# Attention and two MoE layers on one core: the second batch's x and the weight sums in finer pieces, DVE and ACT of M2(0,1) ordered by the scheduler

## The chip, the core and the metric

The kernel runs on one core of a Trainium2 chip. The core has TensorE (PE, the matrix engine), VectorE (DVE), ScalarE (ACT), GpSimd (POOL) and SyncE (SP), which here only issues DMA transfers. Each engine runs its own instructions in order and waits for the others by semaphores. The time is that of one execution on the device, in microseconds (us). The time before is 1480.57 us, the median of 3 runs (1477.91 to 1485.29).

## What is computed

The reference, cut to what matters. There are 8 batches of 576 tokens, 8 heads of 64, so 4608 tokens of width 512; the two layers have a hidden width of 2048.

```python
kv = einsum('bhsd,bhse->bhde', k, v)
out = einsum('bhsd,bhde->bhse', q, kv)
x = out / sqrt(mean(out * out, -1) + 1e-6) * g_norm      # to (4608, 512)

h = x @ moe_w_in
x = (h * sigmoid(1.702 * h)) @ moe_w_out                 # layer l = 0

h = x @ moe2_w_in
x = (h - tanh(h)) @ moe2_w_out                           # layer l = 1
```

## The kernel before

**Stages.** The program goes through the layers l and, in each, through the batches n = 0 to 7. Each pair has two stages: M1(l,n) multiplies the batch's x by w_in and applies the activation into the tiles `GT` (gt_73 to gt_76 in the listings), M2(l,n) multiplies that by w_out. The operands are split into a high and a low f16 part, so every product is three matmuls (high by high, high by low, low by high). In M2 the function `jA` (L811) forms differences of the activation on DVE, `jB` (L825) the high part on ACT, `jC` (L831) the low part on DVE, in seven buffers `JT`.

**Seven products.** M1(0,0), M2(0,0) and M1(0,1) multiply plain 2 x 2 blocks (`m1_plain`, `m2_plain`). From M2(0,1) on the blocks are combined as in Strassen's method: seven products in place of eight. M2 then has 28 steps of 12 matmuls. Its weights come from DRAM by `stream` (L852): one transfer of 512 KB for each two steps, in four buffers `st`, issued by SP; stream 5 holds steps 8 and 9, stream 6 steps 10 and 11.

**The weights of layer 0** come as 64 bit words and are turned into floats and f16 parts by `conv0`. The combinations that the seven products want are formed by `sums`: `four` (L176 to L179) makes four sums or differences, ACT casts them, `low_part` (L182) makes the low f16 part. Eight groups `sums_in` (wi_63 to wi_70) belong to w_in. While a stage still reads the old content of a block, its new high and low part wait in `mscratch`, and `settle` stores them by a transfer of SP (L269).

**The weights of layer 1** are turned by `conv1` (called `later`), which `add_side(later, 0.72, 0.0)` starts at M1(0,2): loads by POOL's queue (L149, L150), words by ACT (L161) and DVE.

**Attention.** The x of the next batches is made beside the matmuls: `front_early` and `back_early` for batches 1 and 2 (during M2(0,0) and M1(0,1) to M2(0,1)), `front` and `back` for the later ones. L445 is the product of k and v, copied to `kv` by ACT (L446); L454 its product with q; `back_early` scales by the root (L648, a product of 128x1152) and `xprep0` or `xprep` makes the high (ACT, L370) and low parts (DVE, L373, L359) in `xo`.

**What sets the order.** These side works are generators. A stage calls `tick` after each step, and each side work then advances by its rate in yields per step. Until the end of M2(0,1) the order of PE, SP, DVE and ACT is the order in which the code is written (`start`, a manual schedule of these four); from M1(0,2) on only PE, SP and POOL are ordered so, and a scheduler orders DVE and ACT.

Of the kernel before, what the change touches and what calls it, by code (L numbers as in the profile page):

```python
# [22 lines left out]
H = T // 2  # L23
# [60 lines left out]
def body(ctx, tc, att, atp, gn, con, w_in, w_out, w2_in, w2_out, outT):  # L84
# [13 lines left out]
    scr = Scratch(scratch, SCRATCH)  # L98
    rx, rs, rq0, rq1, rk = (Scratch(scratch[:, a:z], z - a) for a, z in
                            ((0, 8 * H), (8 * H, 12 * H), (12 * H, 16 * H), (12 * H, 20 * H), (16 * H, SCRATCH)))  # L100
    xk = [Scratch(t.rearrange("p a b c d -> p (a b c d)").bitcast(F32), 14 * H) for t in xo]
# [68 lines left out]

    def four(Q, E, l=0):
# [4 lines left out]
        tt(out=o[0], in0=q21, in1=q22, op=ALU.add)  # L176
        tt(out=o[2], in0=q11, in1=q21, op=ALU.subtract)
        tt(out=o[1], in0=o[0], in1=q11, op=ALU.subtract)
        tt(out=o[3], in0=q12, in1=o[1], op=ALU.subtract)  # L179

# [34 lines left out]
    def conv1():  # L215

        items = [(kind, p, h) for kind in (0, 1) for p in range(NP) for h in range(2)]
        R = [cbk[:, 0:1024], cbk[:, 1024:2048]]
        wb = cbk[:, 2048:3072]
        B = wb.rearrange("p (s f) -> p s f", s=8)  # L220
        load_words(1, *items[0], R[0])
        for _ in range(4):
            yield
        for k, (kind, p, h) in enumerate(items):
            if k < 31:
                load_words(1, *items[k + 1], R[(k + 1) % 2])
            yield from words(1, R[k % 2], wb)
            four(B[:, 0:4], B[:, 4:8], 1)
            yield
            yield  # L230
            d = R[k % 2][:, 0:896].bitcast(F16).rearrange("p (s t f) -> p s t f", s=7, t=2)
            for a, b in ((0, 4), (4, 7)):
                nc.scalar.copy(out=d[:, a:b, 0, :], in_=B[:, 1 + a:1 + b])
                yield
            low_part(d, B[:, 1:8])
            yield
            if kind == 0:
                nc.gpsimd.dma_start(out=wid[p, :, h], in_=d)
            else:
                for a, b, c in ((0, 3, 0), (3, 7, 4)):  # L240
                    nc.gpsimd.dma_start(out=wod[1][c:c + b - a, :, p, h].rearrange("r q t f -> q r t f"), in_=d[:, a:b])
            converted[0] += 1
            yield

    def sums_in(p, at):

        d = wi[p]
        Q = at.rearrange("p (h s f) -> p h s f", h=2, s=4)
        four(Q, Q)
        yield  # L250
# [58 lines left out]
    todo_in, todo_out = [], [(p, h) for p in range(NP) for h in range(2)]  # L309
    made, spare, pre = [0, 0], [], []  # L310
    pieces, barred, own = [0], [], []
# [54 lines left out]
    def xprep0(xb, dst):  # L366

        B = xb.ap.rearrange("p (s f) -> p s f", s=4)
# [6 lines left out]
        xb.free()  # L375
        yield
# [90 lines left out]
    def front_early(b):  # L467
# [6 lines left out]
        for kt in range(2):  # L474
            for i in range(2):
# [4 lines left out]
                for _ in range(4 if i == 0 else 1):  # L480
                    yield
            xbs[b, kt] = yield from rx.need(4 * H)
            ex = yield from rs.need(4 * H)
            og, sq = (t.ap.rearrange("p (i j n) -> p i j n", i=2, j=2) for t in (xbs[b, kt], ex))
            for j in range(2):
# [133 lines left out]
    def half(k, dst):  # L619
# [12 lines left out]
        yield  # L632
        yield from xprep0(xbs[0, k], dst[:, k])

    def back_early(b, dst):

        newton(slice(0, P))
        y, t = yt
        y.free()
        nc.gpsimd.dma_start(out=rd[b], in_=t.ap)  # L640
        t.free()
        yield
        yield from broadcast(b, rq0)
        for _ in range(5 if b == 1 else 9):
            yield
        for kt in range(2):
            o, rb = xbs[b, kt].ap, rbs[b][kt]
# [10 lines left out]
    def back(b, dst):  # L658

        for _ in range(8):  # L660
            yield
        x = xbs[b].ap.rearrange("p (k n) -> p k n", k=2)
        for kt in range(2):
            rb = rbs[b][kt]
            nc.vector.scalar_tensor_tensor(out=x[:, kt], in0=rb.ap, scalar=0.375 * SG, in1=x[:, kt], op0=ALU.mult, op1=ALU.mult)
            rb.free()
            yield
        ex = yield from rq1.need(6 * H)
        B = xbs[b].ap.rearrange("p (k s f) -> p k s f", k=2, s=4)
# [22 lines left out]
        xbs[b].free()  # L692
        ex.free()
        if b < NS - 1:
            yield from fetch(b + 1)
# [439 lines left out]
    def start_sums():  # L1135
# [7 lines left out]
        spare.extend(own + stp + late)  # L1143
        dfr.append(add_side(sums(), 2.4, 4.0))

# [5 lines left out]
    for l in range(2):  # L1151
        for n in range(NS):
            bk = fr = None
            if l == 0:
                if n == 0:
                    bk = add_side(both(1, xo[1]), 0.58, 1.08)
                elif n == 1:
                    bk = add_side(both(2, xo[0]), 1.05, 0.85)
                elif n < NS - 1:
# [24 lines left out]
            if (l, n) == (0, 0):  # L1184
# [9 lines left out]
                def at_step(k):  # L1194
# [7 lines left out]
                    elif k == 14:  # L1202
                        rate(dfr[0], 2.4, 1.0)

# [10 lines left out]
            if (l, n) == (0, 1):  # L1215
# [89 lines left out]
```

## Time and profile before

| what | value |
|---|---|
| median of 3 runs | 1480.57 us |
| profiled execution | 1476.77 us, span 1474.7 us |
| mean granted clock of TensorE | 0.993 |
| M1(0,0), M2(0,0) | 31.5 to 92.7, to 144.2 us |
| M1(0,1), M2(0,1) | 144.2 to 207.6, to 253.2 us |
| M1(0,2) and M2(0,2) | 253.2 to 349.1 us |
| PE, DVE, ACT, POOL busy | 97%, 78%, 60%, 11% of the span |

The stages' bounds are the times at which TensorE begins with the next stage's matmuls; the first six matmuls of a stage stand among the last ones of the stage before it. The time of an execution is longer than its span by what lies around it, here 2.1 us. [...]

### The profile page before, as it was taken

The numbers are of one execution on the slowest core, as the hardware profiler recorded it, in microseconds if no ns is written. First come the engines' busy times: TensorE is split into PE (matmuls) and PEld (weight loads), VectorE is DVE, ScalarE is ACT, GpSimd is POOL, SyncE is SP. The second block draws the span as 40 slices with busy tenths as digits, with TensorE's granted clock in tenths as the row PEclk, the third lists the DMA queues.
The fourth block names the chain that finished last, engine by engine and source line by source line (L and its number), as shares of the span: only waits on it lengthen the run. The fifth ranks groups of instructions, "written<-read, shape, count | busy, mean of one in ns | idle before, by whom it ended". The sixth has DMA issues, their size and how long they took to land.

```text
span 1474.7 us, 30115 instructions
## 1 busy us (share of the span) xinstructions
PE 1428.3 (97%) x11922; PEld 1108.3 (75%) x11922; DVE 1143.9 (78%) x2210; ACT 879.5 (60%) x1918; POOL 168.2 (11%) x262
## 2 busy tenths in 40 slices
PE   7989998999999999999999999999999999999999
PEld 5767676677677777777777777777777777777777
DVE  4996778596895968959799887878687777878485
ACT  5775564665756657657585655556464655555463
POOL 1322010121121202222011100000000000000000
PEclk9999999999999999999999999999999999999999
DMA  8998875357275483765697443341606142332504
GB/s 311 312 349 244 271 246 192 121 168 284 95 245 221 160 293 96 237 225 154 193 322 267 128 145 129 104 154 55 219 16 195 56 153 96 114 120 65 169 15 161
DMA packets 105437, 261.72 MB, mean 177 GB/s; under 512 B 11376, under 2 KB 50928, under 8 KB 105296
## 3 DMA queue, kind: packets, MB, share of 16 engines
q1 hardware_dynamic: 82848, 174.60, 35.7%
q0 software_dynamic: 22448, 85.20, 17.3%
q8 instruction: 93, 1.52, 0.4%
q14 instruction: 48, 0.39, 0.1%
HBM read 208.13 MB, written 51.36 MB: 176 GB/s over the span
## 4 chain that ended last, share of the span: by engine, by line
PE 64%; DVE 15%; issue 8%; DMA 7%; ACT 6%; POOL 1%; SPq 0%; DVEq 0%; ACTq 0%; POOLq 0%
PE X L750 6%; PE X L934 6%; PE X L936 6%; PE X L935 6%; PE X L752 5%; PE X L751 5%; DVE jt L831 3%; PE Z L750 3%; PE Z L752 3%; PE Z L751 3%; PE Y L934 3%; PE Y L936 3%; PE Y L935 3%; DMA x2d<-mscratch 2%; DVE gt L811 2%
## 5 line engine op out<-in xcount | busy, mean ns | idle before, releaser
L825 ACT ACTIVATE jt<-gt 128x576 f16<-128x576 f32 x420 | 284.9, 682 | 181.1 <-DVE jt L831 40.4
L831 DVE SCALAR_TENSOR_TENSOR jt<-gt,jt 128x576 f16<-128x576 f32 x420 | 311.4, 752 | 74.0 <-ACT jt L825 72.6
L934 PE MATMUL X<-jt,st 128*128 128x288 f16 x960 | 275.3, 287 | 4.8 <-ACT mscratch L879 4.6
L935 PE MATMUL X<-jt,st 128*128 128x288 f16 x960 | 275.2, 287 | 0.5 <-DVE jt L831 0.4
L936 PE MATMUL X<-jt,st 128*128 128x288 f16 x960 | 275.3, 287 | 0.0
L750 PE MATMUL X<-xo,wi 128*128 128x288 f16 x896 | 256.6, 286 | 5.9 <-ACT mscratch L783 5.7
L752 PE MATMUL X<-xo,wi 128*128 128x288 f16 x896 | 256.4, 286 | 0.0
L751 PE MATMUL X<-xo,wi 128*128 128x288 f16 x896 | 256.3, 286 | 0.0
L935 PEld LDWEIGHTS <-st 128*128 128x128 f16 x1680 | 164.6, 98 | 50.8 <-issue 9.4
L936 PEld LDWEIGHTS <-st 128*128 128x128 f16 x1680 | 164.6, 98 | 45.6 <-issue 4.0
L934 PEld LDWEIGHTS <-st 128*128 128x128 f16 x1680 | 164.5, 98 | 44.8 <-DMA st<-wod 3.2
L750 PEld LDWEIGHTS <-wi 128*128 128x128 f16 x1568 | 153.4, 98 | 52.9 <-issue 13.8
L751 PEld LDWEIGHTS <-wi 128*128 128x128 f16 x1568 | 153.5, 98 | 46.6 <-issue 8.5
L752 PEld LDWEIGHTS <-wi 128*128 128x128 f16 x1568 | 153.5, 98 | 38.9
L811 DVE TENSOR_TENSOR gt<-gt 128x576 f32<-128x576 f32 x240 | 176.1, 750 | 1.4 <-ACT gt L757 1.0
L783 ACT COPY mscratch<-X 128x288 f32<-128x288 f32 x336 | 133.4, 398 | 73.1 <-PE X L752 66.4
L788 DVE TENSOR_TENSOR mscratch<-Z,mscratch 128x288 f32<-128x288 f32 x224 | 101.6, 454 | 61.1 <-ACT mscratch L783 29.7
L934 PE MATMUL Y<-jt,st 128*128 128x288 f16 x480 | 137.3, 286 | 2.4 <-ACT jt L825 1.2
L935 PE MATMUL Y<-jt,st 128*128 128x288 f16 x480 | 137.2, 286 | 2.0 <-DVE jt L831 2.0
L936 PE MATMUL Y<-jt,st 128*128 128x288 f16 x480 | 137.3, 286 | 0.0
L750 PE MATMUL Z<-xo,wi 128*128 128x288 f16 x448 | 128.6, 287 | 0.0
L752 PE MATMUL Z<-xo,wi 128*128 128x288 f16 x448 | 128.4, 287 | 0.0
(250 smaller groups left out, 2485.8 us busy)
## 6 DMA issues: line engine op xcount, KB each, us to landing
st<-wod SPq DMA_DIRECT2D x210, 512.0 KB, 4.7
xo<-atp POOLq DMA_DIRECT2D x20, 640.0 KB, 8.1
scratch<-x2d SPq DMA_DIRECT2D x32, 288.0 KB, 5.3
cbk<-w_in POOLq DMA_DIRECT2D x32, 256.0 KB, 3.3
cbk<-w_out POOLq DMA_DIRECT2D x32, 256.0 KB, 4.0
scratch<-atp POOLq DMA_DIRECT2D x14, 576.0 KB, 7.2
scratch<-rd POOLq DMA_DIRECT2D x28, 288.0 KB, 6.8
x2d<-mscratch SPq DMA_DIRECT2D x28, 288.0 KB, 6.7
```

The lines of the kernel that those rows point to most:

```text
L750: nc.tensor.matmul(out=out, lhsT=wh, rhs=xh, start=fresh and kt == 0, stop=False, skip_group_check=k)
L751: nc.tensor.matmul(out=out, lhsT=wh, rhs=xl, start=False, stop=False, skip_group_check=k)
L752: nc.tensor.matmul(out=out, lhsT=wl, rhs=xh, start=False, stop=kt == 1, skip_group_check=k)
L783: main(nc.scalar.copy(out=b.ap, in_=x))
L788: main(nc.vector.tensor_tensor(out=b.ap, in0=add[0], in1=b.ap, op=ALU.add))
L811: tt = lambda o, a, b: main(nc.vector.tensor_tensor(out=G[:, :, o, :], in0=G[:, :, a, :], in1=G[:, :, b, :], op=ALU.subtract))
L825: main(nc.scalar.activation(out=j[:, :, 0, :], in_=GT[STEPS2[i][1]][:, :, QD[STEPS2[i][0]], :], func=AF.Copy, scale=SX))
L831: main(nc.vector.scalar_tensor_tensor(out=j[:, :, 1, :], in0=GT[STEPS2[i][1]][:, :, QD[STEPS2[i][0]], :], scalar=SX, in1=j[:, :, 0, :], op ...
L934: nc.tensor.matmul(out=out, lhsT=wh, rhs=xh, start=a, stop=False, skip_group_check=k)
L935: nc.tensor.matmul(out=out, lhsT=wh, rhs=xl, start=False, stop=False, skip_group_check=k)
L936: nc.tensor.matmul(out=out, lhsT=wl, rhs=xh, start=False, stop=z, skip_group_check=k)
```

## The change

Pieces. `four` yields between its two halves, `low_part` after each of its parts, and the rate of the sums goes from 2.4 to 2.9 yields per step (2.8 in M2(0,1)). The x of batch 1 goes at 1.5 yields per step of M2(0,0) instead of 1.08. The x of batch 2 and later is prepared for both halves of the width at once (`merged`), for batch 2 at a rate of 0.74 instead of 0.85. In M2(0,1) the manual schedule `start` ends, and only PE, SP and POOL stay in the written order. `later` is added there already, loads its first words, and goes on only when M1(0,2) begins (`waiting`).

```diff
-        four(Q, Q)
-        yield
+        for part_ in range(2):
+            four(Q, Q, half_=part_)
+            yield
...
         for o, x in ds:
             low_part(o, x)
+            yield
...
+        while made[0] < NP:
+            yield
         load_words(1, *items[0], R[0])
+        while waiting:
+            yield
...
-        for _ in range(5 if b == 1 else 9):
+        for _ in range(6 if b == 1 else 9):
...
             if b == 1:
-                yield from xprep0(xbs[b, kt], dst[:, kt])
-            else:
-                ex = yield from rs.need(3 * H)
-                yield from xprep(xbs[b, kt], ex, dst[:, kt])
+                yield from xprep0(o, dst[:, kt])
+        if b == 1:
+            xbs[b].free()
+        else:
+            yield from merged(b, dst, rw)
...
-        dfr.append(add_side(sums(), 2.4, 4.0))
+        dfr.append(add_side(sums(), 2.9, 4.0))
...
-                    bk = add_side(both(1, xo[1]), 0.58, 1.08)
+                    bk = add_side(both(1, xo[1]), 0.58, 1.5)
                 elif n == 1:
-                    bk = add_side(both(2, xo[0]), 1.05, 0.85)
+                    bk = add_side(both(2, xo[0]), 1.05, 0.74)
...
             if (l, n) == (0, 2):
-                drain(dfr)
-                add_side(later, 0.72, 0.0)
+                waiting.clear()
+                rate(later, 0.72, 0.0)
...
-                rate(dfr[0], 2.4, 0.85)
+                rate(dfr[0], 2.8, 0.85)
+                start.close()
+                man.enter_context(tc.manual_schedule(engines=frozenset([ENG.PE, ENG.SP, ENG.Pool])))
+                add_side(later, 0.0, 0.5)
```

`merged` is the body that `back` had for its differences and parts (L668 to L693), now called by both. Line numbers of the kernel after are 8 to 16 higher than those before (L811 becomes L826, L831 L846, L852 L867, L269 L277, L648 L658).

**SP, around the start of M2(0,1), before.** `st<-wod` are the streams, `cbk<-wfd` loads for the sums, `wi<-mscratch` the settles, `x2d<-mscratch` a store of M2(0,1).

```order
L852 DMA st<-wod_92 128x2048 x4
L291 DMA cbk<-wfd 128x1024 x2
L269 DMA wi_68<-mscratch 128x2x256
L269 DMA wi_70<-mscratch 128x2x256
L852 DMA st<-wod_92 128x2048 x5
L916 DMA x2d<-mscratch 128x2x288
```

After, at the same place:

```order
L867 DMA st<-wod_92 128x2048 x4
L299 DMA cbk<-wfd 128x1024 x2
L867 DMA st<-wod_92 128x2048
L277 DMA wi_70<-mscratch 128x2x256
L867 DMA st<-wod_92 128x2048 x4
L931 DMA x2d<-mscratch 128x2x288
```

The settle of wi_68 is gone, and that of wi_70 now stands behind stream 5 and ahead of streams 6 to 9.

**DVE, the last sums group (wi_70), before.** Rows of `cbk<-cbk` are sums, `wi_70<-` and `mscratch<-cbk` low parts of weights, `jt<-` low parts of operands.

```order
L831 SCALAR_TENSOR_TENSOR jt<-gt_75,jt 128x2x288
L831 SCALAR_TENSOR_TENSOR jt<-gt_73,jt 128x2x288
L831 SCALAR_TENSOR_TENSOR jt<-gt_74,jt 128x2x288
L182 TENSOR_TENSOR wi_69<-cbk,wi_69 128x2x3x128
L182 TENSOR_TENSOR wi_69<-cbk,wi_69 128x2x128
L176 TENSOR_TENSOR cbk<-cbk 128x2x128
L177 TENSOR_TENSOR cbk<-cbk 128x2x128
L178 TENSOR_TENSOR cbk<-cbk 128x2x128
L179 TENSOR_TENSOR cbk<-cbk 128x2x128
L182 TENSOR_TENSOR wi_70<-cbk,wi_70 128x2x3x128
L182 TENSOR_TENSOR mscratch<-cbk,mscratch 128x2x128
```

After, the end of the same group (`gt<-gt` are differences, `mscratch<-Y` results of a product, `scratch<-scratch 128x1152` the x of batch 2):

```order
L888 SCALAR_TENSOR_TENSOR mscratch<-Y_84,mscratch 128x288
L826 TENSOR_TENSOR gt_75<-gt_75 128x2x288
L888 SCALAR_TENSOR_TENSOR mscratch<-Y_85,mscratch 128x288
L846 SCALAR_TENSOR_TENSOR jt<-gt_75,jt 128x2x288
L826 TENSOR_TENSOR gt_76<-gt_76 128x2x288
L184 TENSOR_TENSOR wi_70<-cbk,wi_70 128x2x3x128
L658 TENSOR_TENSOR scratch<-scratch 128x1152
L184 TENSOR_TENSOR mscratch<-cbk,mscratch 128x2x128
L846 SCALAR_TENSOR_TENSOR jt<-gt_76,jt 128x2x288
```

Before, the group ends 8 rows behind the run of three `jt` rows; after, 39 rows lie between the same run of three (gt_75, gt_73, gt_74) and the row `mscratch<-cbk`.

**POOL, the first words of layer 1 (`cbk<-w_in`), before.** `scratch<-atp` and `xo_72<-atp` load the attention's inputs of batch 3, `scratch<-rd` brings the roots of batch 2.

```order
L640 DMA rd<-scratch 128x288
L563 DMA scratch<-rd 64x4x288 x4
L390 DMA scratch<-atp 128x1152
L390 DMA xo_72<-atp 128x1280 x3
L390 DMA scratch<-atp 128x1152
L390 DMA xo_72<-atp 128x1280
L149 DMA cbk<-w_in 128x2x256
L150 DMA cbk<-w_in 128x2x256
```

After:

```order
L650 DMA rd<-scratch 128x288
L572 DMA scratch<-rd 64x4x288 x4
L149 DMA cbk<-w_in 128x2x256
L150 DMA cbk<-w_in 128x2x256
L397 DMA xo_72<-atp 128x1280
L397 DMA scratch<-atp 128x1152
```

The first pair of word loads has moved ahead of batch 3's loads, from the start of M1(0,2) into M2(0,1).

## Rows read from the trace of the kernel before

**Rows 1.** The page, first part: busy time, share of the span, instructions.

```profile
PE 1428.3 (97%) x11922; PEld 1108.3 (75%) x11922; DVE 1143.9 (78%) x2210; ACT 879.5 (60%) x1918; POOL 168.2 (11%) x262
```

**Rows 2.** Windows by stage: M1(0,1), M2(0,1), and a later stage of dense matmuls.

```profile
core 0: us, PE busy (x) PEld busy (x) DVE busy (x) ACT busy (x) POOL busy (x), PEclk, DMA share, GB/s
144.20:207.60 63.40, 57.99 (x512) 41.78 (x512) 44.73 (x104) 37.47 (x80) 7.91 (x14) 0.95 0.77 242
207.60:253.20 45.60, 39.12 (x296) 29.39 (x295) 43.84 (x74) 22.72 (x42) 1.89 (x4) 0.96 0.69 230
408.70:442.80 34.10, 33.38 (x272) 26.30 (x271) 33.95 (x58) 19.37 (x35) 7.11 (x12) 1.00 0.80 264
```

**Rows 3.** Timeline of PE: start, length, row, [idle before <- releaser].

```profile
95.72 0.80 PE L445 MATMUL AT<-scratch 128*64 128x64 f32 x20
...
144.24 0.28 PE L962 MATMUL X<-xo,wi 128*128 128x288 f16 x1 [1.27 <-ACT mscratch L1011]
...
147.73 0.40 PE L963 MATMUL X<-xo,wi 128*128 128x288 f16 x1 [0.73 <-DVE xo L373]
...
181.51 0.72 PE L454 MATMUL AT<-scratch,kv 64*64 64x288 f32 x8 [2.88 <-ACT kv L446]
...
244.96 0.28 PE L934 MATMUL X<-jt,st 128*128 128x288 f16 x1 [2.63 <-ACT mscratch L879]
...
259.12 0.29 PE L750 MATMUL X<-xo,wi 128*128 128x288 f16 x1
...
272.60 1.24 PE L454 MATMUL AT<-scratch,kv 64*64 64x288 f32 x8 [2.07 <-ACT scratch L527]
```

**Rows 4.** Windows of 10 us around PE's waits, columns as in rows 2.

```profile
140.00:150.00 10.00, 6.53 (x55) 4.46 (x54) 8.67 (x19) 5.46 (x12) 1.98 (x3) 0.81 0.87 249
180.00:190.00 10.00, 8.49 (x76) 5.51 (x77) 6.50 (x17) 7.67 (x16) 0.00 (x0) 1.00 0.76 261
240.00:250.00 10.00, 6.99 (x43) 4.67 (x42) 9.93 (x18) 4.36 (x8) 0.00 (x0) 0.83 0.32 108
268.00:278.00 10.00, 7.93 (x55) 5.13 (x54) 5.76 (x13) 7.05 (x18) 0.56 (x1) 0.83 0.04 16
```

**Rows 5.** Timeline of DVE around the start of M2(0,1) and within it.

```profile
205.52 2.09 DVE L831 SCALAR_TENSOR_TENSOR jt<-gt,jt 128x576 f16<-128x576 f32 x3
207.53 1.29 DVE L182 TENSOR_TENSOR wi<-cbk,wi 128x768 f16<-128x768 f32 x2
...
209.18 0.42 DVE L177 TENSOR_TENSOR cbk<-cbk 128x256 f32<-128x256 f32 x1
...
212.30 0.42 DVE L182 TENSOR_TENSOR mscratch<-cbk,mscratch 128x256 f16<-128x256 f32 x1
...
225.60 0.81 DVE L873 SCALAR_TENSOR_TENSOR mscratch<-Y,mscratch 128x288 f32<-128x288 f32 x2
...
227.00 1.35 DVE L648 TENSOR_TENSOR scratch<-scratch 128x1152 f32<-128x1152 f32 x1
228.27 0.75 DVE L811 TENSOR_TENSOR gt<-gt 128x576 f32<-128x576 f32 x1
228.94 0.75 DVE L831 SCALAR_TENSOR_TENSOR jt<-gt,jt 128x576 f16<-128x576 f32 x1
```

**Rows 6.** Timeline of SP's queue; neighbours of one line are merged, first start shown.

```profile
203.96 9.45 SPq L269 DMA_DIRECT2D wi<-mscratch  x2
213.50 11.85 SPq L852 DMA_DIRECT2D st<-wod  x5
```

**Rows 7.** The source line L852 from 207 to 262: 14 streams.

```profile
DMA to landing us min/median/max: 3.7/4.3/7.2
```

**Rows 8.** Timeline of ACT, three places.

```profile
98.38 0.19 ACT L446 COPY kv<-AT 128x64 f32<-128x64 f32 x1
...
142.66 0.62 ACT L278 CAST jt<-jt 128x512 f16<-128x512 f32 x1 [1.16 <-DVE jt L179]
...
268.42 0.68 ACT L161 ACTIVATE cbk<-cbk 128x512 f32<-128x512 f32 x1 [1.88 <-DMA cbk<-w_in]
```

More of the change, by code (lines that the diff above doesn't have):

```diff
@@ L98, in body @@
     scr = Scratch(scratch, SCRATCH)
-    rx, rs, rq0, rq1, rk = (Scratch(scratch[:, a:z], z - a) for a, z in
-                            ((0, 8 * H), (8 * H, 12 * H), (12 * H, 16 * H), (12 * H, 20 * H), (16 * H, SCRATCH)))
+    rx, rs, rw, rq0, rq1, rk = (Scratch(scratch[:, a:z], z - a) for a, z in
+                                ((0, 8 * H), (8 * H, 12 * H), (8 * H, 16 * H), (12 * H, 16 * H), (12 * H, 20 * H), (16 * H, SCRATCH)))
     xk = [Scratch(t.rearrange("p a b c d -> p (a b c d)").bitcast(F32), 14 * H) for t in xo]
@@ L169, in words, with four @@
         yield
-    def four(Q, E, l=0):
+    def four(Q, E, l=0, half_=None):
         q22, q11, q12, q21 = (Q[..., (k + l) % 4, :] for k in range(4))
@@ L175, in four @@
         tt = nc.vector.tensor_tensor
[L176 to L179, printed above, removed]
+        if half_ != 1:
+            tt(out=o[0], in0=q21, in1=q22, op=ALU.add)
+            tt(out=o[2], in0=q11, in1=q21, op=ALU.subtract)
+        if half_ != 0:
+            tt(out=o[1], in0=o[0], in1=q11, op=ALU.subtract)
+            tt(out=o[3], in0=q12, in1=o[1], op=ALU.subtract)
     def low_part(d, src):
@@ L309, in body @@
     todo_in, todo_out = [], [(p, h) for p in range(NP) for h in range(2)]
-    made, spare, pre = [0, 0], [], []
+    made, spare, pre, waiting = [0, 0], [], [], [1]
     pieces, barred, own = [0], [], []
@@ L366, in xprep0 @@
     def xprep0(xb, dst):
-        B = xb.ap.rearrange("p (s f) -> p s f", s=4)
+        B = xb.rearrange("p (s f) -> p s f", s=4)
         for a in (0, 2):
@@ L374, in xprep0 @@
                                            in1=dst[:, a:a + 2, 0, :], op0=ALU.mult, op1=ALU.subtract)
-        xb.free()
         yield
@@ L481, in front_early @@
                     yield
-            xbs[b, kt] = yield from rx.need(4 * H)
+            if kt == 0:
+                xbs[b] = yield from rx.need(8 * H)
             ex = yield from rs.need(4 * H)
-            og, sq = (t.ap.rearrange("p (i j n) -> p i j n", i=2, j=2) for t in (xbs[b, kt], ex))
+            og, sq = (t.rearrange("p (i j n) -> p i j n", i=2, j=2)
+                      for t in (xbs[b].ap[:, kt * 4 * H:(kt + 1) * 4 * H], ex.ap))
             for j in range(2):
@@ L632, in half @@
         yield
-        yield from xprep0(xbs[0, k], dst[:, k])
+        yield from xprep0(xbs[0, k].ap, dst[:, k])
+        xbs[0, k].free()
     def back_early(b, dst):
@@ L643, in back_early @@
         yield from broadcast(b, rq0)
-        for _ in range(5 if b == 1 else 9):
+        for _ in range(6 if b == 1 else 9):
             yield
         for kt in range(2):
-            o, rb = xbs[b, kt].ap, rbs[b][kt]
+            o, rb = xbs[b].ap[:, kt * 4 * H:(kt + 1) * 4 * H], rbs[b][kt]
             nc.vector.tensor_tensor(out=o, in0=rb.ap, in1=o, op=ALU.mult)
@@ L651, in back_early, with merged @@
             if b == 1:
-                yield from xprep0(xbs[b, kt], dst[:, kt])
-            else:
-                ex = yield from rs.need(3 * H)
-                yield from xprep(xbs[b, kt], ex, dst[:, kt])
-        yield from fetch(b + 1)
[L658 to L668, printed above, removed]
+                yield from xprep0(o, dst[:, kt])
[3 more added lines that the diff above has]
+            yield from merged(b, dst, rw)
+        yield from fetch(b + 1)
+    def merged(b, dst, reg):
+        ex = yield from reg.need(6 * H)
         B = xbs[b].ap.rearrange("p (k s f) -> p k s f", k=2, s=4)
@@ L693, in back @@
         ex.free()
+    def back(b, dst):
+        for _ in range(8):
+            yield
+        x = xbs[b].ap.rearrange("p (k n) -> p k n", k=2)
+        for kt in range(2):
+            rb = rbs[b][kt]
+            nc.vector.scalar_tensor_tensor(out=x[:, kt], in0=rb.ap, scalar=0.375 * SG, in1=x[:, kt], op0=ALU.mult, op1=ALU.mult)
+            rb.free()
+            yield
+        yield from merged(b, dst, rq1)
         if b < NS - 1:
@@ L1202, in at_step @@
                     elif k == 14:
-                        rate(dfr[0], 2.4, 1.0)
+                        rate(dfr[0], 2.9, 1.2)
                 m1_plain(0, ahead_of, lambda p: some(3), behind)
@@ L1256, in body @@
             man.close()
-            if (l, n) == (0, 1):
-                start.close()
 def kernel(q, k, v, g_norm, moe_w_in, moe_w_out, moe2_w_in, moe2_w_out):
```

## The prediction

> **What bounds the kernel now.** I read the page's first part, then the stages by windows, then TensorE's own waits, and last the engines and the queue that end them. TensorE is busy for 97% of the span [rows 1], so most of the kernel cannot move: stages from M1(0,2) on are a dense row of matmuls, and the pace there is 34.1 us for 272 matmuls, 0.1254 us each [rows 2]. The change touches only the stretch up to about 280 us. There M2(0,1), from 207.6 to 253.2, is bound by VectorE (DVE), which works 43.84 of 45.6 us while TensorE works 39.12 [rows 2]. So the reader should look for TensorE's idle pieces of over 1 us. They are at 144.24 and 147.73 (start of M1(0,1), for an eviction of ACT and for the x of batch 1), 2.88 us at 181.51 (attention of batch 2, for ACT's copy of kv), 2.63 us at 244.96 (M2(0,1)), and 2.07 us at 272.60 (attention of batch 3 in M1(0,2)) [rows 3].
>
> Some of these waits cost twice. [...] A stretch at 0.83 over 10 us gives away 1.7 us.
>
> **The sum, part by part.** All of it against the profiled execution, which took 1476.77 us.
>
> Finer yields and rate 1.5 in M2(0). The work of batch 1 comes earlier. In the program's order TensorE's first L454 group now stands directly behind the second L445 group, and needs ACT's copy of it: L445 ends at 96.5 and the copy at 98.57 [rows 3, 8], a new stall of about 2 us. I count nothing for it: the start of the next stage is set by DVE and ACT (the wait at 144.24 is for ACT), and 2 us of TensorE fit under that. If that cover were gone it would be 2.0, with the clock 3.7 us.
>
> Start of M1(0,1). Before, TensorE started at 144.24 and then waited for x; its eighth matmul ran at 147.73, so an unbroken start would have been at 147.73 - 7 x 0.122 = 146.9, or up to 147.3 at the lower clock. After, x is ready in time, since its DVE passes (one more of 128x1152, four more of 128x576) stand ahead of the last sums instead of behind them. But the evictions that free bank X stand on ACT behind the cast of jt at 142.66, which waits for DVE's sums [rows 8]. Those passes take 1.27 (from 227.00 to 228.27) and four times 0.67 (from 228.27 to 228.94) [rows 5], 3.95 us; up to 0.7 of it falls into an idle time of DVE there. So the cast starts at 145.9 to 146.6, the evictions follow as before 1.58 us behind, and TensorE starts at 147.5 to 148.2: +0.7, bounds +0.2 and +1.3.
>
> M1(0,1). The 2.88 us at 181.51 are a wait for a kv copy that queued behind two casts of the sums; with the sums a group ahead these casts are over. I take -2.5, bounds 0 and -2.9. It is given back at once, though, since what decides next is on DVE.
>
> M2(0,1), the main term. Up to now the order of DVE and ACT was written out by hand; now the scheduler sets it. The last sums group (wi_70) was done right behind a run of three low parts of operands (L831): these end at 207.6, and its own low part is the row at 212.30 [rows 5]. In the scheduler's order 39 instructions stand between the same run of three and the low part that ends the group: 8 sums of 128x256, 14 differences (old L811), 9 low parts (old L831), 4 low parts of weights, 2 products for x (old L648), 2 fma's. By starts in the timeline a sum takes 0.45 (its row 0.42 and the step between), a difference or low part 0.67, two weight lows 1.29, a product 1.27, two fma's 0.81 [rows 5]: 3.6 + 9.4 + 6.0 + 2.6 + 2.5 + 0.8 = 24.9 us. If DVE comes to that point at 207.6 as before (the two differences now ahead of it and the four sums now behind it nearly cancel), the group ends at 232.5 instead of 212.7.
>
> Nobody on TensorE needs wi_70 yet. But the transfer that stores it (L269, now L277) sits in SP's queue, and the queue works in order: before, it was held from 203.96 with stream 5 behind it, which left at 213.50, 0.8 us after the low part's end [rows 6]. After, stream 5 has been put ahead of it, and streams 6 to 9 stand behind it. Stream 6 would be issued at 233.3; the streams of this stage took 3.7 to 7.2 us to land, the median 4.3 [rows 7]. So step 10, which reads stream 6, starts at 237.6.
>
> TensorE would have come there at about 227: three steps of 12 matmuls from 207.6 (4.5), a wait of about 4.5 for the last evictions of M1(0,1), which ACT's new order puts behind two casts (estimated from the casts' place), and seven steps (10.5). It waits some 10.5 us. From 237.6 remain 18 steps and six matmuls of the next stage, 222 x 0.1254 = 27.8, and one stretch of low clock, 1.7: the point that lies at 259.12 before [rows 3] comes at 267.1. **+8.0 us**, which already holds the terms ahead of it.
>
> M1(0,2). The first words of layer 2 are loaded in M2(0,1). Before, ACT waited 1.88 us for them at 268.42 [rows 8], with the attention's squares queued behind it, and TensorE waited 2.07 for these. I take 1.6 off that wait, and the 1.7 us of low clock behind it: **-3.3**, bounds 0 and -3.8. The order of M1(0,2) is the old one from its first steps on, so nothing else comes.
>
> Sum: +8.0 - 3.3 = +4.7, so 1481.5 for an execution like the profiled one. That lies 3.8 under the median of the runs, 1480.57, from which the same sum gives 1485.3; I forecast the middle, **1483.5 us**. A measurement of this kernel tells about 0.5% (7.4 us) from no change.
>
> [...]
>
> **Rivals.**
>
> (a) The settle comes in time. DVE was busy for 44.73 of 63.40 us in M1(0,1) [rows 2], so sums at a rate of 2.9 may bring it to the run of three low parts much earlier. From wi_70 done before 222 on, stream 6 lands before TensorE comes to step 10; below that nothing is gained. Then M2(0,1) is bound by DVE as now and ends up to 1.8 earlier (2.5 - 0.7): -1.8 - 3.3 = -5.1, 1473.6 on the same middle basis. For it: most of the sums' DVE work is unchanged. Against it: 24.9 us of work in a fixed order behind a point that hangs on TensorE's own outputs of M1(0,1).
>
> (b) Slower: DVE loses time between 207.6 and the wi_70 low part. Each idle microsecond of it moves stream 6 and the end of the stage by as much. For it: low parts wait for ACT's high parts, and these for buffers that TensorE frees, while TensorE itself is late here by 4.5 us. Against it: DVE idled only 1.8 of 45.6 us in this stage [rows 2]. From 3 us on it decides (+7.7); 3 to 8 us give +8 to +13, 1487 to 1492. A landing of 7.2 instead of 4.3 would do as much as 2.9 of them.
>
> (c) The early words change nothing: ACT's squares then wait for something else (the copies of the attention at the same place), TensorE still waits 2.07. Then +8.0, 1486.7. For it: the wait at 272.60 is for a row of ACT's attention, not for the words themselves; against it: directly ahead of that row ACT waits for the words' transfer [rows 8].
>
> **How the numbers follow.** Forecast (+3 to +7) 0.40, (a) 0.20, (b) 0.25, (c) 0.15. Slower by over 0.5% are most of (b), half of (c) and a little of the forecast: 0.21 + 0.08 + 0.03 = 0.32. Faster by over 0.5% is less than half of (a), with the clock or DVE better than reckoned, and a rest: 0.10. Within 0.5%: 0.58. The range takes in (a) at its lower end, 1473, and (b) with about 8 us lost at its upper, 1493; by the forecast's own bounds alone it would be 1480 to 1488.
>
> **What would show it.** SP's settle of wi_70 held for some 20 us and ending near 232; stream 6 issued right behind it; TensorE waiting about 10 us at step 10 in M2(0,1), for a transfer; no 2.88 us wait in the middle of M1(0,1); ACT's first words without a wait in M1(0,2), and the clock at 1.00 there. Wrong it is if the settle ends before 222, if the wait at step 10 is for an operand of DVE instead, or if M1(0,2) keeps its 2 us wait.

## The result, and the profile after

The changed kernel takes 1493.44 us (median of 7 runs, 1489.88 to 1498.61), the kernel before 1482.93 (7 runs): it is slower by 10.5 us at the medians. The ratio of the runs is 1.0087 with a 95% interval of 1.0067 to 1.0107, which is 9.9 to 15.9 us. The forecast was 1483.5 us, with a chance of 0.58 for a change of less than 0.5%; 1493 was the range's end. Of the 9.9 us by which it is off, about 4 are its base (1478.7, the middle between the profiled execution and the median of three runs, where seven runs give 1482.93). The rest is the effect: +4.7 was forecast and +10.5 measured.

The page's first part says little: the work is the same, and TensorE's share of a longer span falls by a point.

```profile
PE 1430.5 (96%) x11922; PEld 1110.3 (74%) x11922; DVE 1143.9 (77%) x2206; ACT 880.5 (59%) x1918; POOL 168.3 (11%) x262
```

The windows by stage, columns as in [rows 2]: M2(0,0), M1(0,1), M2(0,1), and ten microseconds around the longest wait.

```profile
94.57:153.37 58.80, 50.42 (x430) 38.48 (x428) 43.59 (x91) 31.34 (x62) 9.38 (x17) 0.98 0.81 256
153.37:214.93 61.56, 59.03 (x512) 42.44 (x512) 38.95 (x93) 34.87 (x74) 6.57 (x11) 0.93 0.73 231
214.93:269.91 54.98, 39.64 (x297) 30.04 (x294) 44.74 (x73) 25.67 (x46) 4.08 (x7) 0.88 0.59 178
240.00:250.00 10.00, 3.17 (x14) 2.01 (x15) 6.64 (x11) 2.52 (x5) 0.00 (x0) 0.51 0.76 220
```

Before, M2(0,0) lasted 51.55 us (92.69 to 144.24), M1(0,1) 63.40 and M2(0,1) 45.60 [rows 2]. So M2(0,0) is 7.25 longer (4.44 for two waits in it, 2.68 for a longer wait at its end), M1(0,1) 1.84 shorter, M2(0,1) 9.4 longer. M1(0,2), from the last matmul of M2(0,1) to the first of M2(0,2), went from 51.16 to 47.44, 3.72 shorter. These four make +11.1, close to the 10.5 between the medians and inside the interval. The two profiled spans differ by 16.6, since this execution also began M1(0,0) 2.0 later and lost 3.7 behind M1(0,2), in code that the change does not touch.

TensorE's waits, as in [rows 3]. Not all lines have moved by 8 to 16: L452 was L445, L453 was L446, L461 was L454, L470 was L463, and L184 was L182.

```profile
100.50 0.71 PE L461 MATMUL AT<-scratch,kv 64*64 64x288 f32 x8 [2.09 <-ACT kv L453]
...
121.20 0.30 PE L1022 MATMUL X<-jt,wi 128*128 128x288 f16 x1 [2.35 <-DVE wi L184]
...
153.37 0.40 PE L977 MATMUL X<-xo,wi 128*128 128x288 f16 x1 [3.95 <-ACT mscratch L1026]
...
178.15 0.85 PE L452 MATMUL AT<-scratch 128*64 128x64 f32 x20 [2.28 <-ACT ms L470]
...
223.90 0.40 PE L949 MATMUL X<-jt,st 128*128 128x288 f16 x1 [3.99 <-ACT gt L991]
...
246.84 0.42 PE L949 MATMUL Z<-jt,st 128*128 128x288 f16 x1 [11.11 <-DMA st<-wod]
...
275.79 0.29 PE L765 MATMUL X<-xo,wi 128*128 128x288 f16 x1
...
282.70 0.72 PE L461 MATMUL AT<-scratch,kv 64*64 64x288 f32 x8
```

The last wait is the one that was forecast at 10.5, and the row at 282.70 stands where 2.07 us were lost before, now without a wait. The point that lay at 259.12 lies at 275.79. The 2.09 was forecast too, but as covered; the 2.35 was not forecast.

DVE, timeline: the roots' step in M2(0,0) with the weight row behind it, a row of sums in M1(0,1), and the run of three low parts with the last low part of wi_70, as in [rows 5].

```profile
119.72 0.46 DVE L606 TENSOR_TENSOR scratch<-scratch,ms 128x288 f32<-128x288 f32 x1 [2.99 <-ACT dummy L511]
120.21 0.46 DVE L607 SCALAR_TENSOR_TENSOR scratch<-scratch 128x288 f32<-128x288 f32 x1
120.59 0.55 DVE L184 TENSOR_TENSOR wi<-xo,wi 128x384 f16<-128x384 f32 x1
...
176.05 0.43 DVE L181 TENSOR_TENSOR cbk<-cbk 128x256 f32<-128x256 f32 x1
...
214.62 2.10 DVE L846 SCALAR_TENSOR_TENSOR jt<-gt,jt 128x576 f16<-128x576 f32 x3 [0.49 <-ACT jt L840]
...
240.03 0.42 DVE L184 TENSOR_TENSOR mscratch<-cbk,mscratch 128x256 f16<-128x256 f32 x1
```

From the end of the run of three (216.72) to the end of that low part (240.45) are 23.7 us; the forecast counted 24.9. What DVE waits for at 119.72 is on ACT, timeline as in [rows 8]: the kv copy, and the two loads of ACT's tables around the roots.

```profile
100.25 0.19 ACT L453 COPY kv<-AT 128x64 f32<-128x64 f32 x1
...
115.96 1.28 ACT L600 ACT_TABLE_LOAD   x1
...
118.19 1.28 ACT L511 ACT_TABLE_LOAD   x1
...
176.56 1.14 ACT L262 CAST wi<-cbk 128x768 f16<-128x768 f32 x2 [2.20 <-issue]
177.60 0.49 ACT L470 ACTIVATE ms<-AT,eps 128x288 f32<-128x288 f32 x1
...
282.61 0.66 ACT L161 ACTIVATE cbk<-cbk 128x512 f32<-128x512 f32 x1
```

The words at 282.61 have no wait in front of them now (1.88 us before). The rows at 176.56 and 177.60 are the new wait of M1(0,1): the eviction `ms`, for which TensorE waits, stands on ACT behind two casts of the finer sums, and these begin only when DVE has made the sums that they read (176.05 to 176.48).

SP, timeline as in [rows 6]:

```profile
218.47 0.32 SPq L867 DMA_DIRECT2D st<-wod  x1
240.48 0.70 SPq L277 DMA_DIRECT2D wi<-mscratch  x1
241.26 2.00 SPq L867 DMA_DIRECT2D st<-wod  x4
```

and its waits in 200 to 262 (us in total, times, longest):

```profile
SPq L277 <- DVE jt L846: 22.3, 1, 22.3
```

Stream 5 leaves at 218.47. Then the queue stands for 22.3 us until the low part has ended at 240.45 (the releaser's name is that of DVE's next row), and stream 6 leaves right behind the settle.

### The profile page after: what moved, and what is told of

The parts are those of the page before. It is cut to its first block, busy times and chain, and to the rows that moved or that the text cites. A ratio compares the mean times of both kernels' runs of the same rounds, so it can differ in the third digit from the quotient of the medians.

```text
span 1491.3 us, 30095 instructions
## 1 busy us (share of the span) xinstructions
PE 1430.5 (96%) x11922; PEld 1110.3 (74%) x11922; DVE 1143.9 (77%) x2206; ACT 880.5 (59%) x1918; POOL 168.3 (11%) x262
## 4 chain that ended last, share of the span: by engine, by line
PE 58%; DVE 15%; DMA 6%; ACT 4%; issue 4%; POOL 0%; SPq 0%; ACTq 0%; DVEq 0%; POOLq 0%
PE X L765 6%; PE X L949 5%; PE X L767 5%; PE X L766 5%; PE X L951 5%; PE X L950 5%; DVE jt L846 5%; DVE gt L826 3%; PE Z L765 3%; PE Z L767 3%; PE Z L766 3%; DMA x2d<-mscratch 3%; PE Y L949 3%; PE Y L951 2%; PE Y L950 2%
## 5 line engine op out<-in xcount | busy, mean ns | idle before, releaser
L846 DVE SCALAR_TENSOR_TENSOR jt<-gt,jt 128x576 f16<-128x576 f32 x420 | 311.4, 751 | 83.0 <-ACT jt L840 81.7
L826 DVE TENSOR_TENSOR gt<-gt 128x576 f32<-128x576 f32 x240 | 175.4, 748 | 1.3 <-ACT gt L772 1.0
```

The costliest lines, as they stand in the source:

```text
L826: tt = lambda o, a, b: main(nc.vector.tensor_tensor(out=G[:, :, o, :], in0=G[:, :, a, :], in1=G[:, :, b, :], op=ALU.subtract))
L846: main(nc.vector.scalar_tensor_tensor(out=j[:, :, 1, :], in0=GT[STEPS2[i][1]][:, :, QD[STEPS2[i][0]], :], scalar=SX, in1=j[:, :, 0, :], op ...
```

## The experiments

All stages are read from the profiled execution of each run; the ratio is to runs of the kernel before beside it. M2(0,1) in this table ends behind its own last matmul and the first six of M1(0,2), the point that lies at 259.12 before. In e4, e15 and e17 these six follow the last matmul of M2(0,1), and the bound is set behind them all the same. M1(0,2) goes from there to the first matmul of M2(0,2).

| run | M2(0,0) | M1(0,1) | M2(0,1) | M1(0,2) | ratio to before (95%) |
|---|---|---|---|---|---|
| before | 51.55 | 63.40 | 51.49 | 51.16 | 1 |
| after | 58.80 | 61.56 | 60.86 | 47.44 | 1.0087 (1.0067 to 1.0107) |
| e1, old pace in M2(0,0) | 51.54 | 64.39 | 61.11 | 47.44 | 1.0043 (1.0026 to 1.0059) |
| e2, settle late | 60.32 | 63.14 | 49.42 | 50.08 | 1.0032 (1.0019 to 1.0046) |
| e3, both | 51.55 | 64.54 | 49.61 | 50.58 | 0.9994 (0.9979 to 1.0009) |
| e4, hand order | 60.06 | 61.21 | 51.96 | 47.43 | 1.0029 (1.0014 to 1.0043) |
| e6, e3 with coarse sums | 51.55 | 67.67 | 50.64 | 47.44 | 0.9968 (0.9953 to 0.9982) |
| e7, e3 without early words | 51.55 | 64.22 | 49.62 | 54.15 | 1.0005 (0.9988 to 1.0021) |
| e8, before + early words | 51.55 | 63.28 | 51.51 | 47.44 | 0.9963 (0.9950 to 0.9977) |
| e9, before + new pace | 58.80 | 59.51 | 51.50 | 49.25 | 1.0032 (1.0015 to 1.0048) |
| e10, after, roots later | 60.83 | 61.02 | 62.45 | 47.44 | 1.0094 (1.0073 to 1.0115) |
| e11, after, roots and x later | 53.25 | 63.80 | 61.31 | 47.44 | 1.0064 (1.0042 to 1.0085) |
| e12, before + useless matmuls | 56.01 | 63.30 | 51.50 | 50.37 | 1.0019 (1.0004 to 1.0033) |
| e15, e8 + kv later | 51.55 | 61.07 | 50.17 | 47.44 | 0.9943 (0.9927 to 0.9959) |
| e16, e6 + kv later | 51.56 | 61.52 | 54.06 | 47.44 | 0.9973 (0.9960 to 0.9985) |
| e17, e15 + settle late | 51.56 | 61.28 | 50.06 | 53.58 | 0.9974 (0.9960 to 0.9988) |

A row is one execution, and two rows can differ by some 1.5 us through the clock alone. In M2(0,0) TensorE waits 2.09 us for the kv copy after and 2.08 in e2. These are the windows behind that wait, columns as in [rows 2], first after, then e2:

```profile
100.00:104.00 4.00, 3.50 (x32) 2.50 (x33) 3.90 (x8) 2.90 (x7) 0.54 (x1) 1.00 1.11 365
100.00:104.00 4.00, 3.84 (x22) 2.11 (x23) 3.93 (x8) 2.57 (x7) 0.54 (x1) 0.57 1.09 365
```

The granted clock in the traces of before and after is 1.00 or 0.50; in after, matmuls of 128x288 begin 0.12 us apart at 1.00 (160.02 to 161.98) and 0.24 at 0.50 (154.76 to 155.97). In e2 its mean over these 4 us is 0.57, which is 0.50 for 3.4 of them, where after has 1.00, and M2(0,0) is 1.5 longer than after. That it is the clock as well in e10 (2.0 longer than after, with waits of 8.5 us against 8.4) and in e4 (1.3 longer) is an estimate from this.

**e1: the pace of M2(0,0) undone.**

```diff
-                    bk = add_side(both(1, xo[1]), 0.58, 1.5)
+                    bk = add_side(both(1, xo[1]), 0.58, 1.08)
-        for _ in range(6 if b == 1 else 9):
+        for _ in range(5 if b == 1 else 9):
```

> The changed kernel, with the pace of batch 1's x in M2(0,0) as before (1.08 yields per step, 5 yields of waiting). Theory A: the two new stalls of TensorE in M2(0,0), 2.09 us for the kv copy and 2.35 us for the low part of wi_70, are paid in full, because the operands at that stage's end are paced by TensorE's own steps. Then M2(0,0) is back at about 51.5 us (58.8 in the changed kernel), M1(0,1) begins with its old waits for x, the time falls by 4 to 6 us against the changed kernel, to a ratio near 1.004 to before, and the 11 us wait in M2(0,1) stays. Theory B, the one of the prediction (these stalls lie under DVE and ACT): the time changes by less than 1 us.

M2(0,0) is back at 51.54 and both stalls are gone; the ratio falls from 1.0087 to 1.0043, some 6.5 us. M1(0,1) has its waits for x back and is 2.8 longer, so the two stages together are 4.4 shorter, which is the length of the two stalls (2.09 and 2.35). M2(0,1) is as long as after. The stalls were not covered.

**e2: the settle behind the last stream.** `settle(p)` at the end of `sums_in` becomes `putoff.append(p)`, and behind M2(0,1):

```diff
             m2(l, n, tails, pre)
+            while putoff:
+                settle(putoff.pop())
             pre.clear()
```

> The changed kernel, with the settle of wi_70 issued by SP behind the last stream of M2(0,1) instead of between streams 5 and 6. Theory A: the settle in SP's queue is the whole of the 11.1 us wait at step 10. Then that wait and its 10.2 us of low clock go, M2(0,1) falls from 55.0 to 44 to 47 us, the time by 8 to 11 us against the changed kernel, to a ratio of 1.000 to 1.003 to before. Theory B: the scheduler's order of DVE is itself the bound, so TensorE waits for operands of DVE instead; then the stage stays above 50 us and the time falls by less than 4 us.

To the first matmul of the next stage M2(0,1) falls from 54.98 to 43.53, 11.4 us; the ratio falls to 1.0032. The timeline of SP has the five streams in one row:

```profile
221.25 17.69 SPq L867 DMA_DIRECT2D st<-wod  x5
239.45 0.37 SPq L931 DMA_DIRECT2D x2d<-mscratch  x1
```

The scheduler's order of DVE is no bound of its own here: with the queue free the stage is shorter than before (49.42 against 51.49). M1(0,2) takes 2.6 of it back, for a reason that e3 shows.

**e3: both edits.**

> The changed kernel with both edits of the two runs before: old pace in M2(0,0), settle behind the last stream. If both are causes of their own, their gains add: 12 to 16 us under the changed kernel, 1 to 5 us under the kernel before (ratio 0.997 to 0.999), from the wait of 2.07 us with its low clock in M1(0,2) and the 2.88 us wait in M1(0,1) that are gone. If the one gain hides the other, it ends within 1 us of the better of the two.

The gains add: 1.0087 to 0.9994, about 14 us. From the kernel before it cannot be told apart (0.9979 to 1.0009), though M2(0,1) is 1.9 shorter there: M1(0,1) is 1.1 longer than before, and M1(0,2) gains only 0.6. TensorE now waits there for an eviction, and ACT, which makes it, waits for the settle. Timelines of TensorE and of ACT:

```profile
271.99 0.28 PE L765 MATMUL X<-xo,wi 128*128 128x288 f16 x1 [2.10 <-ACT mscratch L798]
```

```profile
271.54 0.40 ACT L798 COPY mscratch<-X 128x288 f32<-128x288 f32 x1 [4.11 <-DMA wi<-mscratch]
```

Put off behind the last stream, the settle leaves SP at 260.88 and lands 10.5 us later, and the eviction writes into `mscratch`, which the settle reads. So this edit frees M2(0,1) and charges M1(0,2); in e2 ACT waits 3.62 us for it in the same way.

**e4: DVE and ACT by hand in M2(0,1).**

```diff
-                start.close()
-                man.enter_context(tc.manual_schedule(engines=frozenset([ENG.PE, ENG.SP, ENG.Pool])))
                 add_side(later, 0.0, 0.5)
...
             man.close()
+            if (l, n) == (0, 1):
+                start.close()
```

> The changed kernel, with DVE and ACT ordered by hand to the end of M2(0,1), as before; everything else of the change stays. Theory A (the scheduler's order puts the low part of wi_70 far back, and by this the settle): the low part ends within 8 us of the start of M2(0,1), stream 6 is not held, and the time falls by 8 to 11 us. Rival: the later place of the low part comes from the finer sums and the rates, not from the scheduler; then SP is held here too and the time falls by less than 3 us.

```profile
225.72 0.42 DVE L184 TENSOR_TENSOR mscratch<-cbk,mscratch 128x256 f16<-128x256 f32 x1
```

The wi_70 low part ends at 226.14, 10.6 us behind the stage's start (25.5 after; the theory said 8), the wait for the stream is gone, and the time falls by 8.6 us at the medians (1484.80). TensorE waits 4.22 us for a low part of DVE instead. So the scheduler's order is needed for the long wait. It does not make it alone: the low part ended 5.1 us behind the stage's start before (hand order, coarse sums), ends 10.6 us behind it here (hand order, finer sums), and 12.3 us in e6 below (scheduler, coarse sums). Only both together give 25.5.

**e7: no early words.** In the kernel of e3, `later` starts at M1(0,2) as before. What the text below calls layer 2 is the layer l = 1.

> The kernel with both edits, with the first words of layer 2 loaded at the start of M1(0,2), as before, not in M2(0,1). Theory A (the prediction's -3.3 us): M1(0,2) goes from 50.6 to 52 to 54 us. Theory B: the gain that the changed kernel showed there (51.2 to 47.4 us) came from the 11 us stall ahead of it, in which ACT and DVE caught up; then M1(0,2) stays within 0.7 us of 50.6.

M1(0,2) goes from 50.58 to 54.15, which is the way of theory A. It does not give the price of the words by itself: TensorE's wait is in both runs the one for the eviction behind the settle (2.10 us in e3, 3.87 here, where the settle took 12.3 us to land), and that is 1.77 of the 3.57 by which M1(0,2) is longer. The clean test is e8.

**e8: the early words alone**, on the kernel before:

```diff
+        while made[0] < NP:
+            yield
         load_words(1, *items[0], R[0])
+        while waiting:
+            yield
...
-                add_side(later, 0.72, 0.0)
+                waiting.clear()
+                rate(later, 0.72, 0.0)
...
                 rate(dfr[0], 2.4, 0.85)
+                add_side(later, 0.0, 0.5)
```

> The kernel before with the early load of the first words alone. Theory A: the wait of 2.07 us at the attention of batch 3 and its low clock go, M1(0,2) falls from 51.2 to about 48 us and the time by 2 to 4 us (ratio 0.9975 to 0.9985). Theory B: the eviction on ACT that the attention waits for is late anyway; M1(0,2) changes by less than 1 us and so does the time.

There is no long stall in this kernel, and M1(0,2) still falls to 47.44, by 3.7 us. The ratio is 0.9963, lower than was expected (0.9975 lies just inside its interval). ACT's words at 266.02 and the numerators behind them start without a wait, timelines of ACT and of TensorE:

```profile
266.02 0.66 ACT L161 ACTIVATE cbk<-cbk 128x512 f32<-128x512 f32 x1
```

```profile
270.53 0.72 PE L458 MATMUL AT<-scratch,kv 64*64 64x288 f32 x8
```

**e9: the pace alone**, e1's edit the other way on the kernel before.

> The kernel before with the new pace of batch 1's x in M2(0,0) alone (1.5 yields per step, 6 yields of waiting). Theory A: the pace alone makes both stalls of TensorE in M2(0,0), M2(0,0) goes from 51.5 to 58 to 60 us and M1(0,1) loses its waits for x (2.2 us and more); the time rises by 3 to 6 us, ratio 1.002 to 1.004. Theory B: the finer sums are needed for it; then M2(0,0) stays near 51.5 us.

The same 2.09 and 2.35 us stalls, the same 58.80 us, and M1(0,1) without its waits for x: 3.4 us longer for the two stages, ratio 1.0032. No other part of the change is needed for it. The wait of 3.95 us at the start of M1(0,1) is there too, but with a clock of 1.00 from 149.6 to 158.0, where the changed kernel had 0.50 from 151.46 to 158.29.

**e12: useless matmuls**, at steps 1 and 9 of M2(0,0):

```diff
                 def at_step(k):
+                    if k in (1, 9):
+                        z = wi[0][:, 0, 1, 0, :]
+                        for _ in range(38 if k == 1 else 42):
+                            nc.tensor.matmul(out=(Z if k == 1 else Y)[0][:, 384:512], lhsT=z, rhs=z,
+                                             start=True, stop=True, skip_group_check=True)
```

> The kernel before with matmuls of no use (their results go to unused columns of a bank) put into M2(0,0): 38 of 128 columns at step 1 and 42 at step 9, some 2.1 and 2.35 us, which makes TensorE late by as much as the two stalls did, with no change on DVE and ACT. Theory A (what TensorE loses there is paid in full): M1(0,1)'s unbroken start and the time move by 3.5 to 4.5 us, ratio 1.0024 to 1.0031. Theory B (the prediction: 2 us and more fit under DVE and ACT): less than 1.5 us.

```profile
100.08 2.30 PE L1198 MATMUL Z<-wi 128*128 128x128 f16 x38
...
127.97 2.51 PE L1198 MATMUL Y<-wi 128*128 128x128 f16 x42
...
152.33 0.28 PE L962 MATMUL X<-xo,wi 128*128 128x288 f16 x1 [1.27 <-ACT mscratch L1011]
```

With the work of DVE and ACT unchanged M2(0,0) is longer by 4.46, all that was put in (the first two rows come to 4.81, but the matmul behind the first of them begins at 102.22, 0.16 before that row's end); M1(0,1) is 0.1 shorter. The last row is the one that stands at 144.24 before [rows 3], with the same wait of 1.27 us for ACT. On ACT's timeline the cast ahead of that eviction has moved as well, from 49.97 us behind the start of M2(0,0) (142.66 in [rows 8]) to 54.43, with the same wait for DVE:

```profile
150.75 0.62 ACT L278 CAST jt<-jt 128x512 f16<-128x512 f32 x1 [1.16 <-DVE jt L179]
```

So DVE and ACT came late by as much as TensorE did. This is the direct test of "covered", and nothing is covered. The second group of matmuls stands some 5 us later in the stage than the 2.35 us stall. The ratio moved less than theory A says (1.0019, with 1.0024 inside the interval): M1(0,2) is 0.8 shorter (50.37 against 51.16).

**e10: the roots later.**

```diff
         yt[:] = y, t
+        for _ in range(2 if b == 1 else 0):
+            yield
         roots(slice(0, P))
```

> The changed kernel, with the roots of batch 1 (two loads of ACT's tables around two activations) two yields later in M2(0,0), so that the last low part of wi_70 stands ahead of the roots' two steps on DVE again. Theory A: the wait of 2.35 us of TensorE for that low part goes, and as the stage's end is paced by TensorE's steps, M2(0,0) falls from 58.8 by 2 to 3 us and the time by as much; the 2.09 us wait for kv stays. Theory B: x of batch 1 is later by the same and the start of M1(0,1) takes it back: less than 1 us.

It does not tell A from B: the 2.35 us stall went, but the product for x on DVE came to its place before the roots had landed, and the sums behind it waited with it. TensorE's wait at the start of M1(0,1) grew from 3.95 to 5.93. Timelines of DVE and of TensorE:

```profile
137.97 1.36 DVE L660 TENSOR_TENSOR scratch<-scratch 128x1152 f32<-128x1152 f32 x1 [3.05 <-DMA scratch<-rd]
```

```profile
155.14 0.40 PE L979 MATMUL X<-xo,wi 128*128 128x288 f16 x1 [5.93 <-ACT mscratch L1028]
```

TensorE's waits in M2(0,0) come to 8.5 us against 8.4 after, so nothing was gained; the 2.0 us by which the stage is longer are not in its waits.

**e11: roots and x later**, e10 with `range(9)` yields before x.

> The changed kernel, with the roots of batch 1 two yields later and its x three yields later, so that x's first product on DVE does not wait for the roots' transfer (3.05 us when the roots alone were moved). Theory A: the 2.35 us stall of TensorE is paid in full as the 2.09 us one is, so M2(0,0) falls from 58.8 to 54 to 57 us and the time by 2 us or more against the changed kernel, unless M1(0,1) then waits for x (up to 2.2 us, told by its length). Theory B: with the sums behind x on DVE the stage's end stays where it was, 58 us or more.

Only the kv wait is left within the stage, and M2(0,0) is 53.25, that is 51.55 + 1.70:

```profile
101.75 0.71 PE L461 MATMUL AT<-scratch,kv 64*64 64x288 f32 x8 [1.73 <-ACT kv L453]
```

M1(0,1) has its x waits back (63.80), and the two stages together are 3.3 shorter than after. So the second stall was paid too. The ratio, 1.0064, is about 3.4 us under that of the changed kernel, though the two intervals overlap.

**e6, e16: coarse sums** (e3 with the sums' old pieces and rates 2.4), and with the last numerators of batch 2 two yields later:

```diff
-                for _ in range(4 if i == 0 else 1):
+                for _ in range(4 if i == 0 else 3 if (b, kt) == (2, 1) else 1):
```

> The kernel with both edits (old pace in M2(0,0), settle behind the last stream), and the sums in the old, coarse pieces at the old rates (2.4). In that kernel M1(0,1) has lost its 2.88 us wait but has two others, 2.28 us for the squares' eviction and about 2 us for an attention load. Theory A: these come with the finer sums, so M1(0,1) goes from 64.5 back to about 63.4 us and the time changes by -1 to 0 us. Theory B: they come from something else, and coarse sums only bring the 2.88 us back: +1 to +3 us.

> The same two yields on top of the kernel with coarse sums, early words, old pace in M2(0,0), settle behind the last stream, DVE and ACT of M2(0,1) by the scheduler. The wait of 3.06 us in M1(0,1) goes, so does the low clock behind it: M1(0,1) from 67.7 to 62 to 64 us, and the time by 2 to 5 us under that kernel, ratio 0.9935 to 0.9955 to before. Rival: M2(0,1) gets longer by as much, since DVE sets its end; then the ratio stays at 0.997.

In e6 the two new waits of M1(0,1) are gone and a wait of 3.06 is back, with 6.8 us of low clock around it. M1(0,2) is 3.1 shorter, for a reason that neither theory has: with the coarse sums the settle of wi_70 is not behind the last stream in spite of the edit, but between streams 5 and 6, as it is after. Timelines of DVE and of SP:

```profile
225.42 0.43 DVE L184 TENSOR_TENSOR mscratch<-cbk,mscratch 128x256 f16<-128x256 f32 x1
```

```profile
216.69 0.33 SPq L865 DMA_DIRECT2D st<-wod  x1
225.88 0.64 SPq L275 DMA_DIRECT2D wi<-mscratch  x1
231.31 6.20 SPq L865 DMA_DIRECT2D st<-wod  x4
```

The low part ends 12.3 us behind the stage's start, TensorE has no wait of over 0.5 us for a stream in M2(0,1) (10.34 in e1, from which this kernel then differs by the pieces and rates of the sums alone), and nothing is charged to M1(0,2). Whether the time falls against e3 is open: the two intervals overlap, and the profiled executions took 1480.22 and 1480.11 us. In e16 the wait of 3.06 is 1.14, M1(0,1) falls to 61.52, a little more than expected, and M2(0,1) gives half of it back by a longer wait for ACT (6.04 in e6), the rival's side:

```profile
222.20 0.40 PE L947 MATMUL X<-jt,st 128*128 128x288 f16 x1 [9.43 <-ACT gt L989]
```

**e15, e17: e8 with the same two yields**, and with the settle of wi_70 put off as well.

> The kernel before with the early words, and the last numerators of batch 2's attention in M1(0,1) two yields later, so that TensorE comes to them after the two casts of the sums on ACT. If the 2.71 us wait there costs what it lasts, M1(0,1) falls from 63.3 to about 61 us and the time by 1 to 2.5 us against the early words alone (ratio about 0.995 to before). If M2(0,1), bound by DVE, takes it back (x of batch 2 is later), the time stays within 0.7 us of the early words alone.

> The kernel before with the early words, batch 2's last numerators two yields later, and the settle of wi_70 behind the last stream. In the same kernel without the last edit a wait of 4.49 us for a stream stands in M2(0,1), with 6.83 us of low clock behind it. Theory A: it is the settle again, here in the hand-written order, that holds the stream; then the wait goes, M2(0,1) falls from 49.4 by 1 to 5 us, less what DVE takes back as the stage's next bound, and the time comes to a ratio of 0.991 to 0.994. Theory B: the stream waits for TensorE or for another transfer; then the wait and the time stay.

e15 is the fastest of all at the medians, 0.9943, below both kernels (its interval meets that of e8). Its wait in M1(0,1) is 0.98 in place of 2.71; in M2(0,1) a wait of 4.49 for a stream has come, which e8 does not have. Timeline of TensorE:

```profile
186.62 0.72 PE L458 MATMUL AT<-scratch,kv 64*64 64x288 f32 x8 [0.98 <-ACT scratch L492]
...
222.92 0.42 PE L938 MATMUL Z<-jt,st 128*128 128x288 f16 x1 [4.49 <-DMA st<-wod]
```

e17 shortens that wait to 1.67, but not the stage (50.06), where TensorE now waits 2.80 us for an eviction of ACT. M1(0,2) is 6 us longer, with this wait in it; timelines of TensorE and of ACT:

```profile
265.68 0.28 PE L754 MATMUL X<-xo,wi 128*128 128x288 f16 x1 [4.44 <-ACT mscratch L787]
```

```profile
265.23 0.40 ACT L787 COPY mscratch<-X 128x288 f32<-128x288 f32 x1 [6.58 <-DMA wi<-mscratch]
```

So in the hand-written order the settle held the stream for a part only, and the 6 us are the price of the late settle, as in e3: 4.44 for the wait and 1.7 for 3.4 us of low clock behind it (matmuls 0.24 us apart from 266.10 on).

## Why the prediction was wrong

**M2(0,0): the step that failed.** "I count nothing for it: the start of the next stage is set by DVE and ACT ... and 2 us of TensorE fit under that." They do not. M2(0,0) is as long as TensorE's own work plus its waits (e12: 4.46 more for 4.46 put in; e11: 1.70 for a stall of 1.73; e9: the pace alone). What misled was the wait at 144.24 for ACT [rows 3]: ACT and DVE are last there, but their own work in M2(0,0) follows TensorE step by step, so a delay of TensorE goes through them and comes out at the end. e12 shows it: with TensorE 4.46 us later the cast and the eviction of ACT are 4.46 us later too, and the wait for them is still 1.27. Of this the prediction had the bound (2.0, with the clock 3.7) and took the wrong end of it.

**The second stall** was missed. The new pace also moved the roots one step ahead. On DVE their two products stand ahead of the last low part of wi_70, which TensorE needs, and wait 2.99 us for ACT's table loads. 2.09 + 2.35 = 4.44 us, and the prediction had 0.

**Start of M1(0,1): +0.7, right.** The wait for the eviction grew from 1.27 to 3.95 (+2.68), the waits for x (1.47 and 0.73) are gone (-2.20): +0.5.

**M1(0,1): -2.5, wrong, of little account.** The 2.88 us wait is gone, but 2.28 us for `ms` behind two casts of the finer sums took its place, with 3.41 us at a granted clock of 0.50 (178.77 to 182.18). e6, where the sums are coarse, has the old wait again and not the new one. The prediction had taken this gain as given back at once and let M2(0,1) begin at 207.6; without the two stalls it began 1.0 us later than that.

**M2(0,1): +8.0, right in its mechanism and nearly in size.** Against the stage's start: stream 6 issued at 25.7 forecast and 26.3 measured, landed at 30.0 and 31.9 (5.6 us instead of 4.3), TensorE at step 10 at 19.4 and 20.8, its wait 10.5 and 11.11, the wait for the evictions 4.5 and 3.99. The stage grew by 9.4. e2, e4 and e6 show the links: with the settle elsewhere the wait is gone, with the hand-written order too, and with the coarse sums as well. Of the clock of 0.50, granted from 240.21 to 250.45, most fell into the wait itself; its part from 246.84 to 250.45 cost 1.8 us, and 1.7 were reckoned, from the mean of 0.83 over 10 us in [rows 4]. The other waits of the changed kernel differ: 0.50 was granted from 178.77 to 182.18 at the 2.28, from 151.46 to 158.29 at the 3.95 and from 223.14 to 226.55 at the 3.99, while the clock was 1.00 from 86.61 to 151.46, across the 2.09 and the 2.35. Other executions have such waits the other way round (2.08 in e2 with a mean of 0.57 behind it, 3.95 in e9 with 1.00), so for waits of 2 to 4 us the runs here give no rule.

**M1(0,2): -3.3, right** (-3.72; in e8, the early words alone, -3.72 too). Rival (c) is out, and so is (a): the low part ended at 240.45, not before 222. Rival (b) named the right sign for a wrong reason: DVE lost no time up to the low part, for which it took 23.7 us where 24.9 were counted. It idled 10.2 us in the stage, but behind that.

The +8.0 was the shift of the point at 259.12. Without the stalls and the later start of M2(0,0), that point moved by 10.35: 1.0 for the later start of M2(0,1), 1.9 because TensorE had stream 6 that much later, -0.5 behind it. So the same sum gives 4.7 + 4.4 for the stalls + 2.4 here - 0.4 in M1(0,2) = 11.1, which is what the four stages show. More than half of what was missing is the step in M2(0,0).

## What to carry to other kernels

An engine that waits last at the end of a stage need not have slack all through it: ask whether its own work follows the other engine step by step, and if so count each stall of that engine in full (4.46 us for 4.46 put in, in e12). When the order of an engine is handed to a scheduler, look for transfers that wait for one of its late rows in a shared queue: what stood behind one here waited too, 22.3 us, though it needed nothing of that row. Before such a transfer is moved further back, ask who waits for the buffer that it empties (ACT here, 4.11 us in e3). And a change made of several parts is best tried part by part: here one part alone, the early load, makes the kernel faster by 0.4%, and the others together took back more. The finer sums and the scheduler's order were not run each alone on the kernel before, so their own prices stay open.

## What the runs showed that was not expected

M1(0,2) lasts 47.44 us, to within 0.01, in nine of these runs: all that load the words early and do not issue the settle behind the last stream. It is longer only where the words come late (before, e9, e12) or where the settle is put off behind the last stream (e2, e3, e17, and e7, which has both). So what looked like one stage giving back the gain of another was the cost of the edit itself, paid one stage later.

Moving the roots later by two yields removed a stall of 2.35 us and gained nothing (e10), because their neighbour, paced by a fixed count of yields, then met a transfer that had not landed.
